# Packing the last quad of heads two and five steps later, and two row tiles of layer 1 loaded in the other order

## The chip, the cores and the metric

The kernel runs on one core of a Trainium2 chip. The metric is the device time of one execution in microseconds (us), lower being better. The engines are TensorE (PE in the profile; its weight loads are PEld), VectorE (DVE), ScalarE (ACT), GpSimd (POOL) and SyncE (SP). SyncE computes nothing: it issues the transfers (DMAs) between HBM and on-chip memory, one after the other in the order of the program.

## The reference

Four layers are run one after the other on x of 2048 rows and 640 columns: attention, Fourier mixing, attention, Fourier mixing. Each adds its result to x.

```python
x = A_x
x = x + _A_ref(_layernorm(x, axis=-1), A_wqkv, A_wo)
x = x + _B_ref(_layernorm(x, axis=-1), B_dft_seq_re, ...)
x = x + _A_ref(_layernorm(x, axis=-1), A_wqkv, A_wo)
x = x + _B_ref(_layernorm(x, axis=-1), B_dft_seq_re, ...)
```

`_A_ref` is attention with 32 heads of 20 columns, where row i looks at rows i - 255 to i; `_B_ref` multiplies by cosine and sine matrices along the 640 columns (real and imaginary part) and along the 2048 rows, and keeps the real part.

## The kernel before

**Attention (layers 0 and 2).** The rows are cut into 16 blocks of 128, the heads into eight quads of four. A step is one block of one quad, so there are 128 steps for all heads (`heads`). Three things run staggered in a step: the score matmuls and row maxima for block s = step + 10 (`s_head`, lines 633 and 638), the transposed scores and the exponentials for block t = step (lines 661 and 671, two instructions of line 671 a step), and the product with the values for block step - 1 (line 696). Every fourth step the row maxima of four blocks are transposed (line 646), copied by ScalarE (line 649) and sent by a transfer into an extra row of `qp` (line 651); the transposed scores of block t read them four steps later.

Behind and between these, TensorE works off other products in portions (`fill`): first the rest of the projection to queries and keys (`project`, line 259 with `wc` among its operands). Its results go through ScalarE and GpSimd (lines 546, 554, 213), are stored to HBM in `qk_d` (line 526), and come back in another layout: `pack` loads one quarter (512 rows) of one quad into the tiles `kp` and `qp`, with 12 transfers of 80 KB (line 596), six for `kp` and then six for `qp`. `heads` issues three of the 12 at once and three at the start of each of the next three steps (`defer(i // 3, f)`). The quad uses one of two pairs of tiles, so the last quad (number 7) overwrites what quad 5 used.

When a quarter is packed is written in the list `due`: for quad q and quarter j it is taken up once s has reached 16 q + 4 j - 8, which is eight blocks before the block that first reads it; for the last quad it is 16 q + `LAST_DUE[j]`, with `LAST_DUE = (-10, -7, 2, 6)`. Since s = step + 10, its four quarters are begun in steps 92, 95, 104 and 108, and their first readers are the score matmuls of steps 102, 106, 110 and 114. Each entry also names how much of the projection must be done by then, counted in units of which the whole has 600, and the portions of line 259 in each step are as large as the most pressing of these demands or the end at step 96 (`ROWS_AT`) asks for.

When the projection is used up, `prepare(4)` begins to load the row tiles of x into the buffer `big` (`load_y`, line 954), which the projection has read until then. These are needed by the next product that TensorE works off, the partial output product of the first 24 heads (`partials`, line 259 with `big` on both sides): after two steps' worth of matmuls VectorE adds the tile of x to the result (line 980). For that product the attention's results are loaded again (lines 861 and 867).

All transfers are issued by SyncE in the order in which the program emits them. A transfer that waits holds all behind it. `sm`, `o_d` and `r_d` (lines 713, 714, 719) are the sums, results and reciprocal sums that each four blocks send off.

**Fourier mixing (layers 1 and 3).** Its second part, `fourier`, is the column product: eight groups of two row tiles each. Groups 1 to 5 of layer 1 (1 to 7 of layer 3) run through `seven`, seven half-size products of line 1729 in place of eight, whose results VectorE and GpSimd add to the two row tiles of x (line 1664). In the code of `seven`, x11 and x12 are the halves of tile 2g, x21 and x22 those of tile 2g + 1. The first product to touch a tile of x is the second one (`t1`, to x22, so tile 2g + 1), the next is the third (`b21`, to x11, so tile 2g). A tile is loaded by `load_x` (line 1653), stored by `store_x` (line 1661), and its place is one of five buffers that also hold other things; a load waits for the store that frees its buffer. In layer 1 the preparation of layer 2 runs along (`more` is true), and from group 4 on `rows_after` loads only the even tile of the next group; the odd one follows at the start of the group.

Of the kernel before, what the change touches and what calls it, by code (L numbers as in the profile page):

```python
# [32 lines left out]
AHEAD_X = 4  # L33
AFTER = 4
ROWS_AT = 96
LAST_DUE = (-10, -7, 2, 6)
FIRST = 7
LATE = 9
BACK = 2
# [26 lines left out]
class Net:  # L66
# [541 lines left out]
    def heads(self, xsrc, xdst, hook):  # L608
# [98 lines left out]
        def finish(quad, bk):  # L707
# [10 lines left out]
            def store():  # L718
# [8 lines left out]

        due = [(16 * q + (4 * j - AHEAD if q < NQ - 1 else LAST_DUE[j]),
                ((-(-160 * (q + 1) // P) - 1) * NSB + 2 * (j // 2) + 2) * per_piece, q, j)
# [865 lines left out]
    def fourier(self, xsrc, xdst, more):  # L1595
# [53 lines left out]
        def load_x(*ts):  # L1649
            for t in ts:  # L1650
                if t < NB and t not in raws:
                    raws[t] = self.raw()
                    nc.sync.dma_start(raws[t], xsrc[t * P:(t + 1) * P, :])

        def rows_after(g):
            load_x(2 * g + 2)
            if not more or g < 4:
                load_x(2 * g + 3)

        def store_x(t):  # L1660
            nc.sync.dma_start(xdst[t * P:(t + 1) * P, :], raws.pop(t))
# [24 lines left out]
        def eight(g, z):  # L1686
            t = 2 * g + z
            for n in range(2):
                if z:
                    coming(g + 1, n)  # L1690
                elif g:
                    self.cut_part(self.quarter(g, n, 1))
            if z == 0:
                if g:
                    self.load_u(g + 1, 1)
                    self.load_u(g + 2, 0)
                if more and g == 6:
                    before(11)
            before(t)
            ops = [self.made.popleft() for _ in range(2)]  # L1700
            for hf in range(2):
                p = self.bank("y", 320)
                cs = slice(hf * 320, (hf + 1) * 320)
                self.all3(p, [((ops[k // KC][0][k % KC], ops[k // KC][1][k % KC]),
                               (wc[k][0][:, cs], wc[k][1][:, cs])) for k in range(2 * KC)])
                add(nc.vector, raws[t][:, cs], p, raws[t][:, cs])
                if z and hf:
                    differences(g + 1)
            store_x(t)

        def seven(g, halfway):
# [29 lines left out]
            self.cut_part(a21)  # L1741
            self.load_u(g + 1, 1)
            rows_after(g)
            halfway()
            product(y, "t2")
# [19 lines left out]
        def before(t):  # L1765
            if not more:
                return
            if t == 8:
                self.tmp = cuts(self.take_qk("kp", 0, F32), D)
                self.home = [self.home[i] for i in (2, 3, 0, 1)]  # L1770
            if 8 <= t < 11:
                for k in range(2):
                    self.prep_load(xdst, 2 * (t - 8) + k)
                if t < 10:
                    self.load_chunk(t - 8)
            i = t - 12
            if 11 <= t < NB - 1:
                for k in range(2):
                    self.prep_stats(2 * i + 2 + k)
                for k in range(2):  # L1780
                    self.prep_norm(2 * i + 2 + k)
            if t == NB - 1:
                self.prep_stats(8)
                self.prep_norm(8)

        def behind(t):
            if more and t >= 12:
                i = t - 12
                if i < 2:
                    self.cut_chunk(i)  # L1790
                for k in range(2):
                    self.prep_turn(2 * i + k)
                if i < 3:
                    for k in range(2):
                        self.prep_load(xdst, 6 + 2 * i + k)
# [15 lines left out]
        self.leave()  # L1811
        self.u_sum = [self.slot_tile(n, 512, F32)[:, :320] for n in ("rr1", "rr2", "vq2")]
        for g in range(NB // 2):
            load_x(2 * g + 1)
            if g in sevens:
                before(2 * g)
                seven(g, lambda: before(2 * g + 1) if g < 5 else None)
            else:
                rows_after(g)
                for z in range(2):  # L1820
                    eight(g, z)
                    behind(2 * g + z)
# [73 lines left out]
```

## Time and profile before

| what | before |
|---|---|
| median of 3 runs | 2179.72 us (2177.11 to 2182.58) |
| the profiled execution, its time | 2178.74 us |
| its span, first to last instruction | 2177.0 us |
| mean granted TensorE clock | 0.997 of full speed |
| layer 0, steps 97 to 101 | 422.6 to 447.2 us |
| layer 1, column product, groups 1 to 5 | 990.4 to 1069.5 us |
| layer 2, steps 97 to 101 | 1508.9 to 1533.7 us |

How to read the rows of the profile: a row of the timeline or of a group names the engine, the line of the kernel, the operation, and what it writes and reads (out<-in). An engine's name with a q behind it (SPq) stands for its instruction queue: issues and waits. In brackets stands how long the engine had been idle before, and what ended that. A transfer in the chain of waits (DMA out<-in) has the time from its issue to its landing.

### The profile page before, as it was taken

The numbers are of one execution on the slowest core, as the hardware profiler recorded it, in microseconds if no ns is written. First come the engines' busy times: TensorE is split into PE (matmuls) and PEld (weight loads), VectorE is DVE, ScalarE is ACT, GpSimd is POOL, SyncE is SP. The second block draws the span as 40 slices with busy tenths as digits, with TensorE's granted clock in tenths as the row PEclk, the third lists the DMA queues.
The fourth block names the chain that finished last, engine by engine and source line by source line (L and its number), as shares of the span: only waits on it lengthen the run. The fifth ranks groups of instructions, "written<-read, shape, count | busy, mean of one in ns | idle before, by whom it ended". The sixth has DMA issues, their size and how long they took to land.

```text
span 2177.0 us, 48902 instructions
## 1 busy us (share of the span) xinstructions
PE 2105.7 (97%) x17812; PEld 1774.9 (82%) x17812; DVE 1625.7 (75%) x3973; ACT 1138.3 (52%) x2131; POOL 919.7 (42%) x1538
## 2 busy tenths in 40 slices
PE   7999999899999999999999999998899999999999
PEld 7987777677868888889999877776778888888899
DVE  6358888776898879786761588887868968687776
ACT  3117777656554545552341277776566645455432
POOL 3037777765513232321230377767655032331222
PEclk9999999999999999999999999999999999999999
DMA  5556666675656564757645566667855454546653
GB/s 184 176 162 191 197 189 200 204 232 165 206 188 216 177 228 160 256 186 271 209 156 172 161 191 198 189 203 202 233 157 185 141 180 135 173 135 229 240 205 136
DMA packets 234288, 414.78 MB, mean 191 GB/s; under 512 B 40768, under 2 KB 87360, under 8 KB 234048
## 3 DMA queue, kind: packets, MB, share of 16 engines
q1 hardware_dynamic: 234048, 411.66, 58.8%
q8 instruction: 141, 2.31, 0.4%
q14 instruction: 99, 0.81, 0.1%
HBM read 283.77 MB, written 126.62 MB: 189 GB/s over the span
## 4 chain that ended last, share of the span: by engine, by line
PE 81%; DVE 8%; DMA 4%; ACT 3%; issue 3%; POOL 1%; SPq 0%; ACTq 0%; DVEq 0%; POOLq 0%
PE banks L1419 29%; PE banks L259 13%; PE banks L241 13%; PE banks L1729 8%; PE banks L696 7%; PE banks L661 6%; PE banks L633 5%; DVE banks L638 1%; DVE qp L234 1%; ACT pt L671 1%; PE banks L343 1%; DMA kp<-qk_d 1%; PE banks L646 1%; DMA x_d<-x 0%; DVE big L980 0%
## 5 line engine op out<-in xcount | busy, mean ns | idle before, releaser
L638 DVE CUSTOM_DVE_ANT_0 banks<-banks,mask 128x384 f32<-128x384 f32 (+2 forms) x1024 | 527.0, 556 | 112.1 <-PE banks L633 94.7
L671 ACT ACTIVATE pt<-banks 128x768 f32<-128x768 f32 (+2 forms) x512 | 393.6, 771 | 176.4 <-PE banks L661 82.7
L677 POOL TENSOR_SCALAR_AFFINE_SELECT pt<-pt 128x256 f32<-128x256 f32 x512 | 219.0, 428 | 217.4 <-ACT pt L671 197.8
L259 PE MATMUL banks<-big,wc 64*128 64x512 f32 x1920 | 272.5, 394 | 0.4 <-DVE pt L444 0.4
L661 PE MATMUL banks<-qp,kp 61*128 61x384 f32 (+2 forms) x1024 | 209.5, 380 | 32.3 <-DVE mc L638 26.8
L696 PE MATMUL banks<-pt,vq 128*32 128x128 f32 x5760 | 210.4, 277 | 3.5 <-ACT pt L671 3.5
L633 PE MATMUL banks<-kp,qp 60*128 60x384 f32 (+2 forms) x1024 | 209.6, 351 | 1.9 <-DVE mc L638 1.8
L259 PEld LDWEIGHTS banks<-big,wc 64*128 64x128 f32 x1920 | 187.9, 185 | 21.3 <-DVE pt L444 0.5
L228 ACT ACTIVATE qp<-pt 128x512 fp32r<-128x512 f32 (+1 forms) x200 | 123.1, 625 | 135.0 <-DVE pt L1350 54.0
L681 POOL TENSOR_SCALAR_AFFINE_SELECT pt<-pt 128x256 f32<-128x256 f32 x448 | 187.6, 419 | 0.0
L661 PEld LDWEIGHTS banks<-qp,kp 61*128 61x128 f32 x1024 | 108.0, 184 | 95.6 <-DVE mc L638 73.1
L234 DVE TENSOR_TENSOR qp<-pt,qp 128x512 fp32r<-128x512 f32 (+1 forms) x198 | 155.9, 796 | 38.2 <-ACT qp L228 36.4
L696 PEld LDWEIGHTS banks<-pt,vq 128*32 128x32 f32 x5760 | 141.6, 109 | 51.6 <-issue 35.7
L1419 PE MATMUL banks<-qp,big 128*128 128x512 f32 x648 | 153.5, 390 | 0.0
L228 ACT ACTIVATE c<-pt 128x512 fp32r<-128x512 f32 x146 | 90.7, 625 | 115.8 <-POOL pt L1328 56.7
L633 PEld LDWEIGHTS banks<-kp,qp 60*128 60x128 f32 x1024 | 126.3, 186 | 25.9 <-DVE mc L638 17.0
L1348 POOL TENSOR_TENSOR pt<-pt,pt 128x512 f32<-128x512 f32 x32 | 46.8, 1461 | 237.8 <-DMA pt<-c 125.9
L638 DVE DVE_READ_ACCUMULATOR2_ANT mc<- 128x1 f32 x1024 | 143.9, 141 | 0.0
L1419 PEld LDWEIGHTS banks<-qp,big 128*128 128x128 f32 x648 | 120.7, 188 | 25.0 <-POOL qp L234 0.9
L234 DVE TENSOR_TENSOR c<-pt,c 128x512 fp32r<-128x512 f32 x144 | 116.6, 812 | 27.1 <-ACT c L228 24.3
L1419 PE MATMUL banks<-qp,xc 128*128 128x512 f32 x480 | 117.6, 391 | 3.8 <-DVE xc L234 2.3
L1419 PEld LDWEIGHTS banks<-qp,xc 128*128 128x128 f32 x480 | 89.5, 188 | 25.4 <-DVE xc L234 5.3
(241 smaller groups left out, 4401.1 us busy)
## 6 DMA issues: line engine op xcount, KB each, us to landing
pt<-c SPq DMA_DIRECT2D x166, 512.0 KB
qk_d<-c SPq DMA_DIRECT2D x80, 512.0 KB
kp<-qk_d SPq DMA_DIRECT2D x384, 80.0 KB
qp<-qk_d SPq DMA_DIRECT2D x384, 80.0 KB
kp<-u_d SPq DMA_DIRECT2D x32, 640.0 KB
o_d<-ou SPq DMA_DIRECT2D x64, 256.0 KB
x_d<-x SPq DMA_DIRECT2D x48, 320.0 KB
v_d<-pt SPq DMA_DIRECT2D x16, 768.0 KB
```

The source lines that it names most:

```text
L228: nc.scalar.activation(hi, src, AF.Copy, scale=-1.0 if neg else 1.0)
L234: (eng or nc.vector).tensor_tensor(out=lo, in0=src, in1=hi.bitcast(F32), op=OP.subtract)
L241: self.nc.tensor.matmul(p, x, y, start=n == 0, stop=n == last)
L259: self.nc.tensor.matmul(ps[a], x[r], y[r], start=half + i == 0, stop=half == 1 and i == n - 1, skip_group_check=True)
L633: nc.tensor.matmul(p, qp[quad % 2][b:b + 60, z, qb * P:(qb + 1) * P], kp[quad % 2][b:b + 60, z, k0 * P:(qb + 1) * P], start=True, stop=True)
L638: nc.vector.tensor_tensor_reduce(out=p, in0=p, in1=self.mask[:, 384 - n * P:], scale=1.0, scalar=NEG, op0=OP.add, op1=OP.max, accum_out=mc ...
L661: nc.tensor.matmul(self.banks[:, banks[e], :n * P], kp[quad % 2][b:b + 61, z, kb * P:(kb + 1) * P], qp[quad % 2][b:b + 61, z, kb * P:(kb + ...
L671: nc.scalar.activation(pt[quad, kb][:, 2 * z:2 * z + 2, :n * P], self.banks[:, b0:b1 + 1, :n * P], AF.Exp, scale=SCALE)
L677: nc.gpsimd.affine_select(out=t[:, :, 0:P], in_=t[:, :, 0:P], pattern=[[0, 2], [1, P]], compare_op=OP.is_ge, fill=0.0, base=0, channel_mul ...
L681: nc.gpsimd.affine_select(out=t[:, :, 256:384], in_=t[:, :, 256:384], pattern=[[0, 2], [-1, P]], compare_op=OP.is_gt, fill=0.0, base=0, ch ...
L696: nc.tensor.matmul(self.banks[32 * h:32 * h + 32, bank, :P], vq[:, 96 * (kb % 4) + 21 * h:96 * (kb % 4) + 21 * h + 32], t[:, h, (qb - kb) ...
L1419: nc.tensor.matmul(self.banks[:, bk, :], p, b[q], start=start and m == 0, stop=stop and last and m == 2, skip_group_check=True)
```

## The change

Two edits. In the first, the deadlines of the last quad's first two quarters move from -10 and -7 to -8 and -2: the first quarter is begun in step 94 in place of 92, the second in step 100 in place of 95. In the second, group 4 of layer 1's column product loads tile 11 in place of tile 10, and the start of group 5 loads tile 10 in place of tile 11 (`load_x` loads only what isn't there yet, so elsewhere the order of loads stays).

```diff
-LAST_DUE = (-10, -7, 2, 6)
+LAST_DUE = (-8, -2, 2, 6)
...
         def rows_after(g):
-            load_x(2 * g + 2)
             if not more or g < 4:
-                load_x(2 * g + 3)
+                load_x(2 * g + 2, 2 * g + 3)
+            else:
+                load_x(2 * g + (3 if g == 4 else 2))
...
         for g in range(NB // 2):
-            load_x(2 * g + 1)
+            load_x(2 * g, 2 * g + 1)
             if g in sevens:
```

## The prediction

> **What bounds the kernel now.** I read the page first: which engine is full, and what the chain that ended last is made of.
>
> ```profile
> PE 2105.7 (97%) x17812; PEld 1774.9 (82%) x17812; DVE 1625.7 (75%) x3973; ACT 1138.3 (52%) x2131; POOL 919.7 (42%) x1538
> PE 81%; DVE 8%; DMA 4%; ACT 3%; issue 3%; POOL 1%; SPq 0%; ACTq 0%; DVEq 0%; POOLq 0%
> ```
>
> TensorE is busy 97% of the span and is 81% of the chain. An edit that takes no matmul away can win only where TensorE stands still or runs at a lower clock. So the second view is the table of stretches, to find those places near the two edits.
>
> ```profile
> 420.00:430.00 10.00, 7.64 (x105) 5.75 (x103) 6.19 (x23) 5.56 (x11) 8.22 (x17) 1.00 0.49 148
> 430.00:440.00 10.00, 5.50 (x58) 4.85 (x60) 4.31 (x14) 1.97 (x4) 1.53 (x4) 0.66 0.99 271
> ```
>
> The columns are PE, PEld, DVE, ACT, POOL, granted clock, DMA share, GB/s. In layer 0, from 428 to 438 us, every compute engine is half idle, the clock is 0.66, and only DMA is full (0.99). Layer 2 has the same hole some 1086 us later. Its size comes from line 671 (two instructions per attention step), counted in stretches:
>
> ```profile
> 422.55:447.15 24.60, 8.12 (x10) 0.86 0.82 244
> 450.95:498.75 47.80, 21.35 (x28) 1.00 0.70 195
> 1508.90:1533.70 24.80, 8.11 (x10) 0.86 0.83 227
> ```
>
> The first and last row are steps 97 to 101 of layers 0 and 2 (ten instructions); the 28 are steps 103 to 116 of layer 0, which do the same kind of work: 47.8 / 14 = 3.41 us a step. Five steps at that pace are 17.1 us, so steps 97 to 101 lose 24.6 - 17.1 = **7.5 us** in layer 0 and 24.8 - 17.1 = **7.7 us** in layer 2. What ends the waits is in the timeline (idle time before an instruction, and its releaser, in brackets) and in the chain in order of time:
>
> ```profile
> 433.09 0.82 DVE L980 TENSOR_TENSOR big<-banks,big 128x640 f32<-128x640 f32 x1 [5.91 <-DMA big<-x]
> ...
> 434.50 0.69 PE L661 MATMUL banks<-qp,kp 61*128 61x384 f32 x2 [5.79 <-DVE mc L638]
> ...
> 435.30 2.60 PE L259 MATMUL banks<-big,big 64*128 64x320 f32 x18
> ...
> 439.82 1.49 PE L259 MATMUL banks<-big,big 64*128 64x320 f32 x18
> ...
> 446.68 0.45 PE L661 MATMUL banks<-qp,kp 61*128 61x384 f32 x2 [0.82 <-DMA qp<-mt]
> ...
> 1519.53 0.82 DVE L980 TENSOR_TENSOR big<-banks,big 128x640 f32<-128x640 f32 x1 [5.54 <-DMA big<-x_d]
> ```
>
> ```profile
> 416.87 3.40 DMA qp<-qk_d
> ...
> 423.17 2.06 DMA qp<-mt
> ...
> 428.32 4.68 DMA big<-x
> ...
> 442.08 4.46 DMA qp<-mt
> ...
> 1515.13 4.30 DMA big<-x_d
> ...
> 1529.52 3.59 DMA qp<-mt
> ```
>
> Line 980 adds the first row tile of x to the first partial product. VectorE takes its work in order, so while it waits 5.91 us for that tile, the score reductions of line 638 behind it wait, and TensorE waits 5.79 us for them. Then 18 matmuls take 2.60 us that later take 1.49: TensorE is slow after the rest. At 446.68 a second transfer is late by 0.82 us, the maxima that line 651 writes into qp.
>
> **Why the tile is late.** It is late at its issue. SyncE (SPq) issues every transfer, in order:
>
> ```profile
> 411.52 1.73 SPq L596 DMA_DIRECT2D qp<-qk_d  x3
> 413.60 1.17 SPq L596 DMA_DIRECT2D kp<-qk_d  x3
> ...
> 415.43 2.03 SPq L596 DMA_DIRECT2D qp<-qk_d  x3
> 417.50 1.09 SPq L596 DMA_DIRECT2D kp<-qk_d  x3
> ...
> 420.00 1.91 SPq L719 DMA_DIRECT2D r_d<-rc  x1
> 421.95 1.12 SPq L596 DMA_DIRECT2D qp<-qk_d  x3
> ...
> 424.29 1.21 SPq L596 DMA_DIRECT2D qp<-qk_d  x3
> 425.54 2.23 SPq L596 DMA_DIRECT2D kp<-qk_d  x6
> ...
> 428.32 1.02 SPq L954 DMA_DIRECT2D big<-x  x2
> ```
>
> ```profile
> L259 PE MATMUL banks<-big,wc x30: 386/392/488, 405.8 to 417.6; 64*128 64x512 f32 x30
> ```
>
> The last projection matmul, after which the buffer of the x tiles is free, starts at 417.6; the load leaves SyncE at 428.32, some 10 us later. Between 411.52 and 428.32 SyncE issues one behind the other, with no rest over 0.5 us between two rows: 24 packing transfers (line 596, all shown) and 7 others, 16.8 us for 31, or 0.54 us each. Every packing transfer ahead of the load delays it.
>
> **Edit 1, the deadlines of the last quad.** A quarter is 12 packing transfers (6 kp, then 6 qp), three a step over four steps. Before, the rows above are: qp of quad 6 (411.52, 415.43); kp (413.60, 417.50) and qp (421.95, 424.29) of the last quad's first quarter, steps 92 to 95; kp of its second (the six at 425.54), steps 95 and 96, whose qp follow in steps 97 and 98. After, the first quarter lies in steps 94 to 97, the second in steps 100 to 103. Nothing is added or removed. The x load stands in the order behind the packing of step 96 and ahead of that of step 97. Ahead of it remain quad 6's six qp and, of the first quarter, the kp of steps 94 and 95 and the qp of step 96: 15 in place of 24, **9 fewer**. Price of one: from below 2.23 / 6 = 0.37 us (issue alone), from above the spacing where SyncE waits for earlier transfers, below (437.44 to 439.66 for three: 0.74 us). Nine are 3.3 to 6.7 us; I take the mean of this very stretch, 0.54, so **4.9 us**. The load then leaves at about 423.4.
>
> ```profile
> 437.44 1.81 SPq L596 DMA_DIRECT2D qp<-qk_d  x3
> 439.66 0.54 SPq L861 DMA_DIRECT2D x<-o_d  x1
> ...
> 447.47 0.38 SPq L719 DMA_DIRECT2D r_d<-rc  x1
> 450.62 1.09 SPq L651 DMA_DIRECT2D qp<-mt  x2
> ...
> 466.08 1.21 SPq L596 DMA_DIRECT2D qp<-qk_d  x3
> ```
>
> VectorE is ready at 433.09 - 5.91 = 427.2. With the old flight of 4.68 us the tile lands at 428.1, a wait of 0.9 us. The flight should shrink too, since fewer transfers are queued right ahead of it; the chain has flights of 2.06 us (423.17) and 3.40 us (416.87) just before. With 3.4 us the tile lands at 426.8 and nothing waits. So 5.0 to 5.9 of the 5.9 us go, and with them the slow matmuls: 2.60 - 1.49 = 1.1 us for one group. What is late next is the maxima of step 98, issued at 442.08: ahead of them the three qp at 437.44 go too (2.2 us), so they leave 4.9 + 2.2 = 7.1 us earlier, at 435.0, and land at 439.4 with the old flight. TensorE wants them in step 102; with all of the 7.5 us gone that is at 446.7 - 7.5 = 439.2. So a wait of a few tenths stays, more if the load leaves later than I say: I put the gain at **6.8 us** in layer 0. In layer 2 the loss is 0.2 us larger, the tile's wait 0.4 us shorter (5.54) and its maxima fly 3.59 us; I take the same 6.8.
>
> [...]
>
> What edit 1 costs: the second quarter's 12 transfers now leave in steps 100 to 103, 12 x 0.37 to 0.74 = 4.4 to 8.9 us of SyncE. After 447.47 + 0.38 SyncE stands idle for 2.8 us, which they fill; 1.6 to 6.1 us of lag remain. Behind them wait the maxima of step 102 (450.62, used in step 106, three and a half steps or 12 us later: covered) and the third quarter, whose last qp leave at 466.08 to 467.29 and, with a flight of 3.4 to 4.5 us, land by 471.8 for use in step 110, which starts near 450.95 + 7 x 3.41 = 474.8: 3.0 us of cover at the longer flight. At the lower price nothing is late; at the upper one about 3 us would be. The second quarter itself has steps 104 and 105 to land, 6.8 us against flights of 2 to 4.7: covered, the same lead that the third has. I take nothing, and keep 3 us per layer for the range. The projection's pace is the largest of the units left over the steps left, to its end (600 units by step 96) and to each deadline (570 by step 92, now 94): with 60 left at step 86 that is 6 a step by the end, 30 / 6 = 5 by the old deadline, 30 / 8 by the new. The end sets it, and no matmul moves.
>
> **Edit 2, tiles 10 and 11 in layer 1.** The column product is bound by TensorE, without idle time but in one place:
>
> ```profile
> 1045.08 0.47 SPq L1653 DMA_DIRECT2D x<-x_d  x1
> 1051.63 1.49 SPq L1661 DMA_DIRECT2D x_d<-x  x2
> 1056.32 0.32 SPq L1653 DMA_DIRECT2D x<-x_d  x1
> 1059.49 0.49 DVE L1664 TENSOR_TENSOR x<-banks,x 128x320 f32<-128x320 f32 x1 [2.42 <-DMA x<-x_d]
> 1060.77 1.73 PE L1729 MATMUL banks<-big,pt 128*128 128x320 f32 x10 [1.76 <-DVE pt L1592]
> ```
>
> Tile 11 is loaded at 1056.32, when the store of tile 8 (1051.63) has freed its buffer. VectorE needs it first in group 5, for x22, and is ready at 1059.49 - 2.42 = 1057.07; TensorE loses 1.76 us. After the edit tile 11 goes at 1045.08, tile 10 at 1056.32. Tile 10 is needed one product later: 15 matmuls at the 1.73 / 10 us of the last row, 2.6 us at most, less the wait that row holds; call it 1.8 us later, 1058.9. It lands at 1059.49 as tile 11 did: VectorE still waits about 0.6 us, but behind that stands only the split for the product after next, one more product (over 1.7 us) away. So TensorE's 1.76 us go; bounds 1.1 (if 0.6 us reaches TensorE) to 2.4 (VectorE's whole wait). No transfer or instruction is added. I take **1.8 us**.
>
> **The sum.** 2 x 6.8 + 1.8 = 15.4 us. The profiled execution took 2178.7 us (span 2177.0); the median of the three runs is 2179.7, so the execution is 1.0 us, or 0.05%, below it. From the first 2163.3, from the second 2164.3; I give **2164**, and count the rivals from the median.
>
> **Rivals.**
> (a) *Only issue time is won*, 3.3 us a layer, the flight stays at 4.68 and the maxima keep the rest: 2 x 3.3 + 1.8 = 8.4, so 2171. For it: DMA is at 0.99 after 430. Against it: it was at 0.49 in 420 to 430, when the load would now fly.
> (b) *The wait comes back later.* DMA share over steps 97 to 101 is 0.82 and over 103 to 116 0.70; 12 transfers of 80 KB added there could make the third quarter 3 us late in step 110 in each layer: 15.4 - 6 = 9.4, so 2170. [...]
> (c) *Slower*: the second quarter at the upper price, 8.9 us, in the dense stretch around step 102. It decides from the point where its lag of 6.1 us passes the cover of 3.0 in step 110 and also holds the maxima and step 114: two waits of 3.1 to 6.1 us with a slow clock after each (1.1), about 10 a layer, against a gain of 3.3 in the poor case (a): 2 x 6.7 - 1.8 = 11.6 slower, 2191. Against it: the idle 2.8 us, and steps 103 to 116 ran at clock 1.00 with the third and fourth quarters spaced just so.
> (d) *It doesn't do what it says*: SyncE is slow there not by the number of transfers but by single ones that hold it (1.91 us at 420.00); the load stays where it was, and only edit 2 counts: 2178. Against it: the packing rows alone are 10.6 of the 16.8 us.
>
> **How the numbers follow.** Forecast 0.64 (own range 2158 to 2168), (a) 0.16, (b) 0.11, (c) 0.04, (d) 0.05. The range goes from 2157 (all of 7.5 + 7.7 + 2.4 us, and 4 for other small waits for SyncE and the runs' scatter) to 2173 (cases a and b with the scatter). About 0.3%, 6.5 us, is what a measurement of this kernel can tell from no change. Faster by more: 0.64 and most of (a) and (b), 0.85. Within: the rest of them and (d), 0.10. Slower: (c) and a little, 0.05.
>
> **What would show it.** In the changed trace the first load of big by line 954 leaves some 4 to 5 us sooner before its reader, line 980 has no idle time over 1.5 us, steps 97 to 101 take 17 to 18.5 us instead of 24.6, and the clock of that stretch is 1.00. At the x22 addition of group 5 the wait of 2.42 us is gone and line 1729 shows no idle time. The forecast is wrong if line 661 or 633 waits for kp or qp transfers in steps 106 to 114, or if line 980 waits as before.

## The result, and the profile after

The changed kernel takes 2170.5 us (median of 6 runs, 2167.9 to 2173.5); the kernel before, run beside it, 2181.5 us (median of 6, 2177.1 to 2185.8). The ratio is 0.9948, with a 95% interval of 0.9935 to 0.9962: 0.52% or 11 us less, where 2164 was forecast, with a range from 2157 to 2173. The execution that was profiled took 2173.5 us (span 2171.7), the longest of the six, so the page shows 5.3 us less than the page of before (2178.7), not 11.

The first rows of the page, to be set beside the two of before: busy time of each engine, and shares of the chain that ended last.

```profile
PE 2108.7 (97%) x17812; PEld 1779.9 (82%) x17812; DVE 1625.0 (75%) x3973; ACT 1138.5 (52%) x2131; POOL 919.2 (42%) x1538
PE 82%; DVE 6%; ACT 4%; DMA 3%; issue 2%; POOL 2%; SPq 1%; ACTq 0%; DVEq 0%; POOLq 0%
```

The count of matmuls is the same; DVE and DMA have each lost a point or two of the chain. The table of stretches of the changed kernel, with the columns of before (PE, PEld, DVE, ACT, POOL, granted clock, DMA share, GB/s), for the twenty microseconds of the old hole:

```profile
420.00:430.00 10.00, 9.24 (x133) 6.68 (x130) 7.54 (x27) 6.70 (x13) 8.67 (x19) 1.00 0.70 191
430.00:440.00 10.00, 8.21 (x130) 7.12 (x126) 8.65 (x29) 5.03 (x9) 5.13 (x13) 1.00 1.03 274
```

In 430 to 440 us TensorE is busy for 8.2 us in place of 5.5 and the clock is 1.00 in place of 0.66. The transfer engines are as full as before (1.03 against 0.99). The next rows are the stretches of steps by line 671's instructions (ACT busy, granted clock, DMA share, GB/s): steps 97 to 101 and 103 to 116 of layer 0, then of layer 2.

```profile
424.15:442.67 18.52, 8.11 (x10) 1.00 0.96 275
446.31:495.19 48.88, 21.35 (x28) 1.00 0.78 215
1505.40:1525.70 20.30, 8.11 (x10) 1.00 0.93 267
1530.90:1578.70 47.80, 21.36 (x28) 1.00 0.77 209
```

Steps 97 to 101 take 18.5 and 20.3 us where they took 24.6 and 24.8. Of these 6.1 and 4.5 us some is lost again. Layer 0's steps 103 to 116 take 1.1 us more (48.88 against 47.80). In layer 2, step 102 lasts from 1525.70 to 1530.90, 5.2 us, against 3.64 before. From step 97 to step 117 the gain is 5.1 us in layer 0 (76.2 to 71.0) and 2.9 us in layer 2 (76.2 to 73.3).

The timeline and the chain show what is left. First layer 0 (an instruction's start, its time, and in brackets the idle time before it):

```profile
424.77 0.85 SPq L954 DMA_DIRECT2D big<-x  x2
...
430.10 0.82 DVE L980 TENSOR_TENSOR big<-banks,big 128x640 f32<-128x640 f32 x1 [1.56 <-PE banks L696]
...
431.51 0.45 PE L661 MATMUL banks<-qp,kp 61*128 61x384 f32 x2 [1.48 <-DVE mc L638]
...
431.97 1.49 PE L259 MATMUL banks<-big,big 64*128 64x320 f32 x18
...
437.37 1.51 SPq L651 DMA_DIRECT2D qp<-mt  x2
...
442.13 0.45 PE L661 MATMUL banks<-qp,kp 61*128 61x384 f32 x2 [1.10 <-DMA qp<-mt]
...
470.90 0.41 PE L633 MATMUL banks<-kp,qp 60*128 60x384 f32 x1 [0.90 <-DMA qp<-qk_d]
```

then layer 2:

```profile
1507.76 0.84 SPq L954 DMA_DIRECT2D big<-x_d  x2
...
1511.75 0.82 DVE L980 TENSOR_TENSOR big<-banks,big 128x640 f32<-128x640 f32 x1 [1.91 <-DMA big<-x_d]
...
1520.62 1.18 SPq L651 DMA_DIRECT2D qp<-mt  x2
...
1525.17 0.45 PE L661 MATMUL banks<-qp,kp 61*128 61x384 f32 x2 [2.48 <-DMA qp<-mt]
...
1525.63 2.90 PE L259 MATMUL banks<-big,big 64*128 64x320 f32 x18
```

and the flights from the chain of waits (time from issue to landing):

```profile
437.37 4.62 DMA qp<-mt
...
1507.76 3.90 DMA big<-x_d
...
1520.62 4.41 DMA qp<-mt
```

The first of two waits is much shorter, the second longer, and a third is new. The tile of x still makes line 980 wait 1.56 and 1.91 us, after 5.91 and 5.54. (The releaser named in layer 0, line 696, is not a reader or writer of that tile. In VectorE's queue the semaphore instruction of line 980, which waits for the tile's transfer, ends at 430.05; the addition starts 5.33 us after the tile's issue.) The maxima of step 98 make TensorE wait 1.10 and 2.48 us, and after the second of these 18 matmuls take 2.90 us in place of 1.49. Before, the maxima were 0.82 us late in layer 0 and 1.35 us in layer 2:

```profile
1533.24 0.45 PE L661 MATMUL banks<-qp,kp 61*128 61x384 f32 x2 [1.35 <-DMA qp<-mt]
```

In layer 0 the third quarter's packing is 0.90 us late in step 110.

In layer 1 the rest at group 5 is gone. The timeline there:

```profile
1043.47 0.47 SPq L1653 DMA_DIRECT2D x<-x_d  x1
...
1054.79 0.32 SPq L1653 DMA_DIRECT2D x<-x_d  x1
...
1057.11 1.92 PE L1730 MATMUL banks<-big,pt 128*128 128x320 f32 x12
...
1057.76 0.49 DVE L1665 TENSOR_TENSOR x<-banks,x 128x320 f32<-128x320 f32 x1 [1.00 <-DMA x<-x_d]
```

Tile 11 now goes out at 1043.47 and tile 10 at 1054.79. VectorE waits 1.00 us for tile 10, and line 1730 (1729 before) has no idle time in this product: its matmuls take 77.1 us from first to last, where they took 78.9.

The sum of the three places is 5.1 + 2.9 + 1.8 = 9.8 us, close to the 11 of the medians. The two profiled executions differ by less (5.3 us) because the later one began 1.6 us late in step 0 and has four short windows outside the changed stretches (at 522, 597, 642 and 1676 us) in which the granted clock is 0.50 for 3.41 us, where the earlier one's is 1.00; the first of them lengthens step 126 by 0.8 us.

### The profile page after: what moved, and what is told of

It reads as the page before. It is cut to its first block, busy times and chain, and to the rows that moved or that the text cites. A ratio compares the mean times of both kernels' runs of the same rounds, so it can differ in the third digit from the quotient of the medians.

```text
span 2171.7 us, 48905 instructions
## 1 busy us (share of the span) xinstructions
PE 2108.7 (97%) x17812; PEld 1779.9 (82%) x17812; DVE 1625.0 (75%) x3973; ACT 1138.5 (52%) x2131; POOL 919.2 (42%) x1538
## 4 chain that ended last, share of the span: by engine, by line
PE 82%; DVE 6%; ACT 4%; DMA 3%; issue 2%; POOL 2%; SPq 1%; ACTq 0%; DVEq 0%; POOLq 0%
PE banks L1419 30%; PE banks L259 13%; PE banks L241 12%; PE banks L1730 9%; PE banks L696 7%; PE banks L661 6%; PE banks L633 5%; DVE banks L638 1%; ACT pt L671 1%; PE banks L343 1%; DMA kp<-qk_d 1%; ACT big L1041 1%; POOL rs L1089 1%; DVE qp L234 1%; PE banks L646 1%
## 5 line engine op out<-in xcount | busy, mean ns | idle before, releaser
L661 PE MATMUL banks<-qp,kp 61*128 61x384 f32 (+2 forms) x1024 | 209.5, 380 | 25.6 <-DVE mc L638 19.5
L1419 PEld LDWEIGHTS banks<-qp,xc 128*128 128x128 f32 x480 | 89.9, 188 | 24.6 <-DVE xc L234 4.3
```

What stands on the lines that cost most here:

```text
L661: nc.tensor.matmul(self.banks[:, banks[e], :n * P], kp[quad % 2][b:b + 61, z, kb * P:(kb + 1) * P], qp[quad % 2][b:b + 61, z, kb * P:(kb + ...
L1419: nc.tensor.matmul(self.banks[:, bk, :], p, b[q], start=start and m == 0, stop=stop and last and m == 2, skip_group_check=True)
```

## The experiments

Each run has its own runs of the kernel before beside it on the same chip; all ratios are to those. The theory to be tested: the second quarter's transfers no longer stand ahead of, and fly together with, the first tile and the maxima. The rivals: it is the first quarter's place, it is the tile's issue time alone, or it is the two row tiles of layer 1.

**The parts alone.** First the new order of tiles with the deadlines of before, and the deadlines with the old order of tiles:

```diff
-LAST_DUE = (-8, -2, 2, 6)
+LAST_DUE = (-10, -7, 2, 6)
```

> Only the tiles of layer 1, old deadlines. My theory: TensorE's 1.76 us of rest at group 5 go and nothing else changes, so 1.8 us (0.08%) less than before, ratio about 0.9992; line 980 waits 5.5 to 6 us as before. Rival (the wait passes from tile 11 to tile 10): the same time as before, and a rest of TensorE on line 1729 stays. The rows of group 5 decide it, the time can hardly.

> Only the deadlines, old order of the tiles. My theory: the whole gain but 1.8 us, so 9 us less than before, ratio about 0.9958. Rival (the edits help each other, or the tiles bring more than their rows show): under 7 us.

The tiles alone: 2181.7 us, ratio 0.9994 (0.9982 to 1.0007). In the trace the column product is 1.8 us shorter (77.1 us) and TensorE waits for nothing in it; a median cannot show that. The deadlines alone: 2173.2 us, ratio 0.9953 (0.9940 to 0.9966), so nearly all of the gain is theirs. In that run's layer 0 line 980 waited only 0.40 us, but the waits of TensorE show in step 110 (in all, times, longest):

```profile
PE banks L633 <- DMA kp<-qk_d: 2.1, 1, 2.1
```

In its layer 2 line 980 waited 3.47 us and TensorE 0.77 us in step 110. The better the start of the stretch went, the later was the third quarter.

**One quarter alone.** The new tile order, with only the second quarter moved, and with only the first:

```diff
-LAST_DUE = (-8, -2, 2, 6)
+LAST_DUE = (-10, -2, 2, 6)
```

> The change, but the first quarter at its old step 92; only the second quarter is late. Theory A (two transfers are late, the first x tile and the maxima of step 98, and the one that ends last sets the gain): ahead of the tile 6 packing transfers go in place of 9, so line 980 waits 1.6 us longer than in the changed kernel, about 3.3 us; ahead of the maxima all 12 go as in the changed kernel, so step 102 starts at the same time; total within 2 us of the changed kernel, 9 to 11 us less than before. Theory B (only the tile counts): two thirds of the gain of the deadlines, 6 + 1.8 = 8 us less.

```diff
-LAST_DUE = (-8, -2, 2, 6)
+LAST_DUE = (-8, -7, 2, 6)
```

> The change, but the second quarter at its old step 95; only the first quarter is late. Theory A: ahead of the tile 3 packing transfers go, 1.6 us; ahead of the maxima none, so they are as late as before and take what the tile gave: 2 to 4 us less than before, of which 1.8 are the tiles of layer 1. Theory B: a third of the gain of the deadlines, 3 + 1.8 = 5 us less.

The second alone: 2171.2 us, 0.9953 (0.9941 to 0.9965), as the whole change. Line 980 waits 2.00 us in layer 0 and 0.41 in layer 2, less than the 3.3 us expected, and TensorE has no wait for the maxima. The first alone: 2181.7 us, 0.9996 (0.9984 to 1.0008), as the tiles alone. Its trace says why. In layer 0 line 980 waits 3.52 us in place of 5.91, so 2.4 us are won there, and then:

```profile
445.92 0.44 PE L661 MATMUL banks<-qp,kp 61*128 61x384 f32 x2 [2.00 <-DMA qp<-mt]
...
446.63 2.94 PE L259 MATMUL banks<-big,big 64*128 64x320 f32 x18
```

In layer 2 line 980 waits 4.32 us in place of 5.54, and TensorE then 3.11 us for the maxima. The maxima take the tile's place: half of the second quarter, its six qp transfers, still leaves between the two, and what the tile won is lost to the maxima and to slow matmuls behind that rest. The move of the first quarter brings nothing by itself, and that of the second is enough. Which half of the second quarter counts, the six kp transfers that stood ahead of the tile or the six qp behind it, was not tried apart.

**Is it the issue time of one transfer?** If so, a transfer that goes out past SyncE's queue should do as well. In the changed kernel ScalarE issues the maxima of step 98; in the kernel before it issues the first tile; and in the changed kernel both:

```diff
 def m_rows(quad, u, bank):
-                self.post(1, lambda z=z: nc.sync.dma_start(
+                self.post(1, lambda z=z, q=nc.scalar if (quad, u) == (NQ - 2, 2) else nc.sync: q.dma_start(
```

> The changed kernel, but the two transfers of the maxima of step 98 are issued by ScalarE, past SyncE's queue. If their place in SyncE's order is the cause (theory A): they leave right after ScalarE's copy, some 7 us sooner, no rest at step 102 for them, 2 to 4 us less than the changed kernel, ratio to before 0.993 to 0.994. Rival (the 16 transfer engines are the limit, whoever issues): they leave sooner but land as late, the rest stays, 0.995.

```diff
 def load_y(self, ts):
-                self.nc.sync.dma_start(self.y_part(t), self.xsrc[t * P:(t + 1) * P, :])
+                (self.nc.scalar if t == 0 else self.nc.sync).dma_start(self.y_part(t), self.xsrc[t * P:(t + 1) * P, :])
```

> The kernel before (old deadlines, old tile order), but the first tile of x is issued by ScalarE, past SyncE's queue, in each attention layer. Theory A: line 980 no longer waits 5.9 us, but the maxima of step 98 are as late as before and take its place, a rest of 4 to 6 us at step 102: at most 2 us a layer less, ratio 0.998 to 1.000. Theory B (only the tile counts): 5 to 7 us a layer less, ratio 0.994 to 0.995. If the transfer engines were the limit, the tile would land as late as before and line 980 would wait as long.

> The changed kernel with both the first tile of x and the maxima of step 98 issued by ScalarE. Theory A: no rest over 0.5 us for either, steps 97 to 101 take 17 us in both layers as they do further on, 5 to 7 us less than the changed kernel (its rests 1.48 + 1.92 + 1.10 + 2.48 us), ratio to before about 0.992. Rival (transfer engines): 0.995 as the changed kernel.

All three lost. The maxima by ScalarE: 2177.5 us, 0.9981 (0.9967 to 0.9994), against 0.9948 for the change. The tile by ScalarE in the kernel before: 2193.6 us, 1.0058 (1.0041 to 1.0076), slower than before. Both in the changed kernel: 2186.0 us, 1.0021 (1.0009 to 1.0034). The transfers in question did leave sooner, in layer 0 and against the start of step 97: in the first run the maxima by 7 us, in the second the tile by 8.6 us, in the third the tile by 3.5 and the maxima by 2.8 us. What they cost stands in the waits of SyncE's queue, in these three runs in turn:

```profile
SPq L596 <- DMA qp<-mt: 5.2, 1, 5.2
```

```profile
SPq L596 <- DMA big<-x: 6.8, 1, 6.8
```

```profile
SPq L714 <- DMA big<-x: 5.9, 1, 5.9
```

The transfers that wait here (packing of line 596, the results of line 714) read neither the maxima's tile `mt` nor `big`, and the maxima of quad 6 go into the other pair of `qp` than the last quad's packing. Yet SyncE stands still until the transfer that ScalarE issued has landed. The semaphores in the traces say why. In the kernel before, the 1972 transfers raise eight semaphores in strict turn (100 to 105, 107 and 109), and 1754 of the issues wait on the very semaphore that their own transfer will raise. The rows above say whose landing raised the semaphore that ended SyncE's wait: that of the transfer which ScalarE had issued. In the first run SyncE comes to these packing issues at 425.03 and takes 6.43 us over the three; ScalarE issues the maxima only at 429.49. So these runs did not give a free way past the queue; they put a rest of 5.2 to 6.8 us into it. In the first run TensorE has no wait for the maxima in step 102, and pays later, in steps 106 and 110 (timeline):

```profile
456.98 0.41 PE L633 MATMUL banks<-kp,qp 60*128 60x384 f32 x1 [1.34 <-DMA qp<-qk_d]
...
474.50 0.66 PE L633 MATMUL banks<-kp,qp 60*128 60x384 f32 x1 [3.86 <-DMA kp<-qk_d]
```

In the second run line 980 no longer waits for the tile, and TensorE rests 6.23 us (layer 0) and 5.00 us (layer 2) for the maxima in step 102: they take the tile's place, as theory A had it, though here SyncE's hold makes them later too. So the three are no clean test of one transfer's issue time. What they do show is that one early transfer is worth little when the rest are later for it.

**Fewer transfers at the crowded place.** In the changed kernel four more tiles of x, 320 KB each, leave SyncE between the first tile and the maxima, and the later of them are not needed so soon. The change with two tiles of x asked for ahead in place of four:

```diff
-AHEAD_X = 4
+AHEAD_X = 2
```

> The changed kernel, but tiles of x are loaded two ahead of the partial product in place of four, so two loads of 320 KB (tiles 3 and 4) fewer stand ahead of the maxima of step 98. If the maxima are late by what is queued ahead of them: about 2.4 us earlier (1.2 us each), TensorE's rests for them at step 102 (1.10 and 2.48 us in the changed kernel) go, 2 to 4 us less than the changed kernel, ratio to before 0.993 to 0.994. If the rest there has another cause: the same as the changed kernel, 0.995.

It takes 2168.3 us (2165.0 to 2169.8), ratio 0.9935 (0.9917 to 0.9953). The stretches of steps 97 to 101 of layers 0 and 2 (line 671, columns as above):

```profile
422.95:439.44 16.49, 8.12 (x10) 1.00 0.97 287
...
1503.09:1519.78 16.69, 8.12 (x10) 1.00 0.96 280
```

Five steps at 3.41 us are 17.1, so nothing is lost here any more, and no rest for the maxima is left. In the change this stretch of layer 0 moved 18.52 us x 275 GB/s = 5.1 MB, here 16.49 us x 287 GB/s = 4.7 MB, both with the transfer engines 0.96 or 0.97 busy. That would fit a stretch which lasts as long as its transfers do, but a longer stretch also takes in more transfers. With four tiles ahead the stretch took as little in two other traces, 16.8 us in layer 0 with the deadlines alone and 16.7 us in layer 2 with the second quarter alone, so these rows do not show what the two tiles are worth. And the third quarter is late in step 110, with slow matmuls behind it (18 in two groups, 1.87 and 1.26 us, where the same groups take 1.04 and 0.60 us some 4.5 us later):

```profile
468.25 0.41 PE L633 MATMUL banks<-kp,qp 60*128 60x384 f32 x1 [1.69 <-DMA qp<-qk_d]
...
468.25 1.87 PE L259 MATMUL banks<-big,big 64*128 64x320 f32 x12
...
469.67 1.26 PE L259 MATMUL banks<-big 64*128 64x320 f32 x6
...
473.06 1.04 PE L259 MATMUL banks<-big,big 64*128 64x320 f32 x12
...
473.94 0.60 PE L259 MATMUL banks<-big 64*128 64x320 f32 x6
```

Whether the deadlines are needed at all once fewer tiles go out was the next question: two tiles ahead with the deadlines of before.

> The changed order of tiles in layer 1 with the deadlines of before, and two row tiles of x asked for ahead in place of four. If the first tile's late issue behind the packing is what counts and what follows it is only its company, the wait of line 980 stays at 4 to 6 us, steps 97 to 101 take 23 us or more and the ratio is 0.9975 to 1.000. If the four tiles' own 1.3 MB in front of the maxima are the load that matters, the deadlines are not needed: steps 97 to 101 take 19 us or less and the ratio is 0.995 or better.

2178.1 us, ratio 0.9985 (0.9972 to 0.9998). Line 980 waits 5.73 and 5.36 us as before, steps 97 to 101 take 23.7 us in both layers; only the wait for the maxima in step 102 is gone. The deadlines carry the gain.

**The third quarter.** Two tiles ahead, with the third quarter a step earlier, and with the second, third and fourth all a step earlier:

```diff
-LAST_DUE = (-8, -2, 2, 6)
+LAST_DUE = (-8, -2, 1, 6)
```

> The change with two row tiles of x asked for ahead in place of four, and besides the last quad's third quarter begun in step 103 in place of 104. In the version with two tiles ahead alone, TensorE stands still for 1.69 us (layer 0) and 0.82 us (layer 2) in step 110 for a qp transfer of that quarter. If that wait is a matter of when its transfers are asked for, a step (3.4 us) more of lead takes it away: no rest over 0.5 us in step 110, steps 103 to 116 at 48.3 us or less in both layers where no half clock falls into them, and some 2 us less than with two tiles ahead alone: ratio 0.9925 to before, 2165 us. If the rest only moves on because the transfer engines are full there, it comes back as a rest of 1 to 2 us in step 106 (maxima or second quarter) or step 114, and the ratio stays at 0.9935 or worse.

```diff
-LAST_DUE = (-8, -2, 2, 6)
+LAST_DUE = (-8, -3, 1, 5)
```

> The change with two row tiles of x asked for ahead, and the last quad's second, third and fourth quarters all begun one step earlier (99, 103, 107). If lead alone decides, no rest over 0.5 us for kp or qp in steps 106, 110 and 114, and the first tile of x, which leaves ahead of step 99's packing, is not touched: steps 97 to 101 at 17 us or less, ratio 0.9925 to before. If the second quarter's earlier start puts its packing ahead of the maxima of step 98 again, TensorE rests 0.5 to 2 us for them in step 102, and the ratio is 0.994 to 0.9955.

The first: 2165.8 us, ratio 0.9932 (0.9914 to 0.9950); the second: 2165.9 us, 0.9929 (0.9913 to 0.9944). In both, the rest in step 110 is gone from both layers and steps 103 to 116 take 47.7 us, the pace of before. So that rest was a matter of lead: a step more takes it away, and nothing is late for it in steps 106 or 114. The medians are 2.5 us under the run with two tiles alone, but the kernel before was 1.7 us faster beside these two runs, so the ratios are hardly lower, and their intervals overlap. In both traces line 980 waits again, 1.2 to 2.2 us. In the first of them, steps 97 to 101:

```profile
422.25:439.70 17.45, 8.12 (x10) 1.00 0.95 268
...
1499.89:1518.17 18.28, 8.12 (x10) 1.00 0.93 266
```

Up to step 103 this program issues the same transfers in the same order as the run with two tiles ahead alone, which needed 16.5 and 16.7 us; so 1 to 1.6 us of this stretch are scatter between executions.

Last, the same with the first quarter back in steps 92 to 95, to take that last wait away:

```diff
-LAST_DUE = (-8, -3, 1, 5)
+LAST_DUE = (-10, -3, 1, 5)
```

> As the run with the second, third and fourth quarters a step early and two row tiles ahead (ratio 0.9929), but the first quarter back at its old steps 92 to 95, so that no packing stands in steps 96 to 98. If what is left of line 980's wait there (1.19 us in layer 0, 2.08 us in layer 2) comes from the first quarter's transfers of steps 95 to 97 being in flight around the tile, it falls below 0.5 us in both layers and the ratio to 0.9915 or less. If the first quarter's place is of no weight, as the runs with it moved alone suggest, the wait stays between 0.4 and 2.2 us and the ratio within 0.001 of 0.9929.

A miss: 2168.1 us, 0.9944 (0.9928 to 0.9960). Layer 0 went nearly as hoped (line 980 waits 0.51 us, steps 97 to 101 take 16.5 us), but in layer 2 the wait is 2.19 us and TensorE has a new one:

```profile
PE banks L661 <- DMA qp<-mt: 1.3, 1, 1.3
```

These are the maxima of step 94, used in step 98; the first quarter's packing lies around them again. The interval overlaps those of the two runs before it, so the runs do not settle whether the first quarter is better early or late.

The fastest medians, 2165.8 and 2165.9 us, lie some 14 us under the kernel before. That both beat the kernel before is shown; their ratios, 0.9932 and 0.9929 against the change's 0.9948, have intervals that overlap the change's, so that they beat the change too is only likely.

## Why the prediction was right, and where it was too good

**Bound and place: right.** The time came from steps 97 to 102 of layers 0 and 2 and from group 5 of layer 1, and from nowhere else.

**The issue of the tile (4.9 us sooner): right in layer 0.** The load leaves 0.62 us after the start of step 97, where it left 5.73 us after it: 5.1 us sooner. In layer 2 it is 2.30 against 6.17 us, 3.9 sooner.

**The flight (3.4 to 4.7 us): the first term that was off.** From issue to use it grew in layer 0, from 4.77 to 5.33 us. In layer 2 the flight shrank from 4.30 to 3.90 us, but not to the 3.4 hoped for, and there the issue was 1 us short as well. So 1.56 and 1.91 us of the wait stayed, where 0 to 0.9 were expected, over the limit of 1.5 that the prediction had set. The argument was that fewer transfers are queued ahead of the load. Against it stands that the stretch is shorter, and its transfer engines are 0.96 and 0.93 busy, where they were 0.82 and 0.83 over the longer one; that this is what keeps the flights long was not shown apart.

**The maxima (a few tenths of wait): off in the same way.** They leave 13.2 us after the start of step 97 in place of 19.5 in layer 0 (6.3 sooner, 7.1 expected) and 15.2 in place of 20.6 in layer 2 (5.4). Their flights became longer, 4.62 and 4.41 us after 4.46 and 3.59, and they are 1.10 and 2.48 us late, where they were 0.82 and 1.35 us late before. In layer 2 this rest brought the slow matmuls back, 2.90 - 1.49 = 1.4 us for one group.

**The cost of the second quarter (nothing; 3 us a layer kept): nearly right.** TensorE waits 0.90 us in step 110 of layer 0 and not at all there in layer 2. The place was the one that rival (b) and the last part of the prediction had named, at a third of its price in one layer. The prediction had named such a wait of line 633 as a sign that its forecast is wrong. With the deadlines alone it was 2.07 and 0.77 us, and with two tiles ahead 1.69 and 0.82: this cover of 3 us was thin. In all four stretches of steps 97 to 101 that took under 17 us with the third quarter at its old place, TensorE waited for it, 0.8 to 2.1 us.

**The sum per layer: the step that failed, by size.** 6.8 us per layer became 5.1 and 2.9 in the profiled execution. The two other traces with this move of the second quarter and four tiles ahead give 5.5 and 2.2 (the deadlines alone) and 5.6 and 6.6 (the second quarter alone, steps 97 to 117), so the mean of three is 5.4 in layer 0 and 3.9 in layer 2. With 1.8 for the tiles that is 11.1 us, beside 11.0 by the medians. So close an agreement is luck: single traces scatter by about 2 us in layer 2 (with the old deadlines its steps 97 to 116 took 76.2 us before and 78.1 us in the run with the tiles alone). The forecast of 15.4 had taken nearly the best case of the flight in both layers and the maxima along with it. The measured time lies at the 2171 and 2170 of rivals (a) and (b), in part because the kernel before measured 2181.5 us beside it and not 2179.7; as a gain, 11 us lies between their 8.4 and 9.4 and the 15.4 of the forecast. Each had a piece of it: the flight hardly shrank, and the third quarter was late. As mechanisms neither is right alone: issue time is not all that counts, as the move of the first quarter alone shows (the tile leaves 2.8 and 2.2 us sooner, and the ratio is 0.9996), and the rest in step 110 is far from 3 us.

**What was credited to the first quarter: wrong, though the number fitted.** Nine transfers at 0.54 us were counted, three of the first quarter and six of the second. The first quarter's move alone gives 0.9996, the second's alone 0.9953. The count ahead of the tile was right; that each of the nine is worth its 0.54 us was not. As long as the second quarter leaves between tile and maxima, what the tile wins the maxima lose.

**The clock: half right.** The slow matmuls were to go with the tile's wait, and there they did: after the tile's rests of 1.48 and 1.92 us the 18 matmuls take 1.49 us, where they took 2.60 after a rest of 5.79 us in layer 0 before. But after a rest of 2.48 us in layer 2 they take 2.90 us, at a granted clock of 0.50, and with the first quarter alone 2.94 us after 2.00. The forecast had no slow matmuls behind the maxima.

**The pace of the projection: right.** Steps 92 to 96 take 13.75 us before and after.

**The tiles (1.8 us): right**, 78.9 to 77.1 us, with VectorE's wait of 1.00 us (0.6 expected) reaching nothing.

**Rivals (c) and (d): refuted.** Nothing was late in step 114, and the load moved.

## What to carry to other kernels

When a late transfer holds the critical engine, look at all that share the crowded stretch, and move out what is needed last, not only what stands ahead of the late one: here 12 packing transfers moved behind the maxima were worth the whole gain, while the move that only let the tile out sooner gave it to the next transfer in line. Take flights from stretches as crowded as the new one will be: when a stretch gets shorter and keeps most of its bytes, flights need not get shorter with it (here 4.8 us from issue to use became 5.3 in one layer, and a flight of 4.3 us became 3.9 in the other). After such a move look for the next deadline behind it with a thin cover, and give it a step of lead.

## What had not been expected of the hardware

- Half clock after short rests. 18 matmuls of 1.49 us took 2.90 us after a rest of 2.48 us and 2.94 us after 2.00 us. In another execution (two tiles ahead, third quarter early) a rest of 2.18 us brought none:

```profile
1507.92 0.44 PE L661 MATMUL banks<-qp,kp 61*128 61x384 f32 x2 [2.18 <-DVE mc L638]
...
1508.38 1.35 PE L259 MATMUL banks<-big,big 64*128 64x320 f32 x16
```

  So the length of the rest alone did not decide; what did was not shown. In the changed kernel's execution the rest of 2.48 us lay in 3.42 us with 0.94 us of work by TensorE, and the next 3.41 us ran at 0.50 (PE busy is the first column after the length, the clock stands third from the end):

```profile
1522.25:1525.67 3.42, 0.94 (x21) 0.59 (x13) 0.81 (x4) 1.19 (x3) 1.71 (x4) 1.00 1.00 385
1525.67:1529.08 3.41, 3.41 (x25) 3.08 (x24) 1.11 (x5) 1.00 (x2) 1.46 (x3) 0.50 0.87 249
```

  The rest of 2.18 us lay across two stretches of that length with over 2 us of work in each, and the clock was 1.00 in both:

```profile
1503.47:1506.89 3.42, 2.27 (x36) 1.62 (x32) 1.23 (x5) 1.54 (x4) 2.98 (x7) 1.00 0.90 252
1506.89:1510.30 3.41, 2.38 (x31) 2.12 (x34) 2.82 (x11) 0.93 (x2) 0.76 (x2) 1.00 1.04 233
```

  The amount of work did not decide alone either. In the changed kernel's execution 3.41 us with 1.72 us of it, from 593.83, came ahead of 3.41 us at 0.50, and 3.41 us with 1.66, from 563.11, ahead of 3.42 us at 1.00. From 20.4 us to the last matmul the clock was 0.50 seven times in the executions of the two kernels: for 6.83 us from 431.90 and from 1517.33 us in the kernel before, and for 3.41 us from 522.15, 597.24, 641.61, 1525.67 and 1675.85 us in the changed one. Within each execution these starts lie whole multiples of 3.413 us apart (318; 22, 13, 259 and 44).

- A transfer issued by ScalarE held up SyncE's issues for 5.2 to 6.8 us until it had landed, though what SyncE was to issue does not touch its data: SyncE waited on the semaphore that this transfer raised (in the kernel before, 1972 transfers share eight).
- With the same transfers in the same order, the first tile came in time in one execution (line 980 waits 0.42 us in layer 0) and 1.37 us late in another: it left 0.8 us later after the start of step 97, and took 0.6 us longer to land.
